# Spreading 1/den for every attention block by DMA turns instead of a matmul with a constant

## Chip, cores, metric

One core of one Trainium2 chip. The metric is the device time of one execution in microseconds (us). The kernel before takes 1090.96 us (median of 3 runs, 1089.22 to 1092.67). Engines: PE is TensorE, PEld its weight load, DVE VectorE, ACT ScalarE, POOL GpSimd, SP the engine that issues most DMAs.

## The reference

Four residual layers, bf16, 2048 tokens of width 512 (linear attention, gated MLP, linear attention, gated MLP, the two kinds with shared weights), forward and all gradients. What the change touches is the division by `den`:

```python
def _A_ref(x, wqkv, wo):                     # 32 heads of 16
    q, k, v = ...                            # x @ wqkv
    pq, pk = phi(q), phi(k)                  # where(t > 0, t + 1, exp(t)) + 1e-6
    kv = einsum("bhsd,bhse->bhde", pk, v); z = einsum("bhsd->bhd", pk)
    num = einsum("bhqd,bhde->bhqe", pq, kv)
    den = einsum("bhqd,bhd->bhq", pq, z)[..., None] + 1e-6
    return (num / den)... @ wo
x = x + _A_ref(_layernorm(x), ...)           # layer 0
x = x + _B_ref(_layernorm(x), ...)           # layer 1: (sigmoid(x wg) * (x wu)) wd
...                                          # layers 2 and 3 again, then jax.vjp for all gradients
```

## The kernel before

The tokens lie in 8 blocks of 256. The second pass of an attention layer (`a_p2`) makes, for each block, `den` (32 heads for each token), its reciprocal, the reciprocal spread over the 16 elements of each head and turned to have channels in partitions, the product `pnT = pqT * 1/den` (and `rphiT` for the gradient), then `ya = pnT @ Wp`. `Wp` is the product of the layer's `kvT` and `wo`, needed by all blocks.

There are two ways to spread. Blocks 0 and 1 of layers 0 and 2 (`RDMA = (2, 2)`) go over PE; blocks 2 to 7 go over DMA:

```python
    def den():
        ...                                             # 8 small matmuls into PSUM, + EPS into dn
        if by_dma:
            nc.vector.reciprocal(r[:], dn[:])
            for j in range(2):                          # cast and spread over the 16 elements of a head
                st["rx", j] = s1(k, "rx")
                ...
                if l == 0: nc.scalar.copy(dst, src)
                else:      nc.gpsimd.tensor_copy(dst, src)
            return
        nc.vector.reciprocal(r[:], dn[:])
        st["rr"] = rr = k.rr[k.rr_i % 2]                # bf16 high part and remainder, side by side
        nc.vector.tensor_copy(rr[:, :, 0:H], r[:])
        nc.vector.tensor_tensor(rr[:, :, H:2 * H], r[:], rr[:, :, 0:H], ALU.subtract)

    def turn():                                         # PE path: two transposes, one DVE copy
        for j in range(2):
            nc.tensor.transpose(tps[:, j, :], st["rr"][:, j, :], k.ident[:])
        nc.vector.tensor_copy(st["rT"][:], flat(tps[:]))

    def turn_by_dma(j):                                 # DMA path
        if j == 0: st["rT"] = t2(k, "rTx", [P, 2, NDC, P])
        nc.sync.dma_start_transpose(out=st["rT"][:, j, :, :], in_=st["rx", j][:])

    def spread(hf):                                     # PE path: r_ps is in PSUM
        for c2 in range(2):
            nc.tensor.matmul(ps[:, c2, :], lhsT=k.spread[:, 2 * hf + c2, :], rhs=st["rT"][:], ...)
        nc.vector.tensor_tensor(A.pn[b][:, sl, :], pq[:, sl, :], ps[:], ALU.mult)
        nc.vector.tensor_scalar(ph[:], flat(pq[:, sl, :]), -EPS, 1.0, ALU.add, ALU.min)
        nc.vector.tensor_tensor(flat(A.rphi[b][:, sl, :]), ph[:], flat(ps[:]), ALU.mult)

    def spread_turned(hf):                              # DMA path: the same three with rT in SBUF
        nc.vector.tensor_tensor(by_tile(A.pn[b]), by_tile(A.pq[b]), rT, ALU.mult)
        ...
```

The order of instructions on every engine is not written by hand. A planner builds it before the launch: each piece of work has a priority, the longest way from it to the end, plus an offset from a table; a model of the engines and buffers then gives each free engine its best ready piece. Its estimate of a step:

```python
    HOP = dict(PE=0.25, A=0.14, V=0.14, P=0.14, D=2.2)
    LAP = 0.08
    ...
        u.post = [(e, c if e == "D" else c - self.LAP, marks(m)) for e, c, m in u.post]
    ...
            u.prio += self.offsets.get(...)             # the table OFFSETS, 132 entries
```

## Time and profile before

| | before |
|---|---|
| time, us | 1090.96 |
| span of the profiled execution | 1090.0 |
| PE busy | 97% |
| DVE busy | 59% |
| PE time lost (waits and slow clock) at the start of layer 0's second pass, 45 to 76 us | 5.7 us (worked out below) |

The page, the stretches and the chain are in the prediction. Two more views matter later. First, what PE waits for between 40 and 80 us in the kernel before (waiting line, releaser: us in all, times, longest):

```profile
PE hT_ps L490 <- ACT h L555: 1.3, 1, 1.3
PE ya_ps L926 <- DVE rphiT L919: 1.3, 2, 1.1
```

The waits are several and short: for a DVE product, then for the layer norm `h` of layer 1. Second, where `Wp` is begun (the matmuls of `wp_ps` between 52 and 66 us: shortest, median, longest in ns, first and last start):

```profile
L751 PE MATMUL wp_ps<-wo,kvT x4: 377/379/379, 54.2 to 55.6; 128*128 128x512 bf16 x4
```

**A measure of lost time.** The records of PE's matmuls are incomplete (7292 of 7388 in this trace), so PE's busy time can be off by several us. The weight loads are complete, and each names its matmul. I therefore give every matmul the time it takes at full rate (0.109 us for 256 columns: eight take 0.88 us in the chain) and call the rest of any stretch *lost*: waits and slow clock together. The kernel before has 1055.7 us of work and 34.3 us lost. A recount with slightly different times for the short matmuls moves single entries of the tables below by up to 0.7 us and the differences between two rows by at most 0.4, mostly 0.2.

### The profile page before, as it was taken

The page shows a single profiled execution, that of the slowest core. Times are in us where ns is not written, and L with a number is a line of the kernel's source. Part 1 is how long each engine was busy: PE and PEld are TensorE (multiplying, and loading weights), DVE is VectorE, ACT ScalarE, POOL GpSimd, SP SyncE. Part 2 cuts the span into 40 slices and gives each one's busy share as a digit, 9 for nine tenths or more (in the row PEclk, how much of TensorE's full clock was granted, in tenths as well). Part 3 has the DMA queues.
Part 4 walks back from the last instruction along what each step waited for, and adds up shares of the span by engine and source line. Part 5 has one row for each costly group of instructions (what it writes and reads, how often), then busy time and mean ns, then how long its engine had stood idle before and what let it go on. Part 6 is the DMA issues. An engine that isn't in the chain of part 4 may idle for free.

```text
span 1090.0 us, 19650 instructions
## 1 busy us (share of the span) xinstructions
PE 1057.6 (97%) x7292; PEld 694.3 (64%) x7388; DVE 641.5 (59%) x1571; ACT 357.3 (33%) x713; POOL 184.8 (17%) x459
## 2 busy tenths in 40 slices
PE   6989999999999999999899999989999999999998
PEld 3657667677666766675556556655554466666787
DVE  6797786799885778787767657877755000000010
ACT  6665564455333433232234434331111000000010
POOL 4146675524402112000000000000000000000000
PEclk9999999999999999999999999999999999999999
DMA  7749879997999898866999799789999999999980
GB/s 247 258 136 289 247 221 258 261 206 180 214 225 217 224 213 190 193 160 157 238 249 255 216 272 273 207 191 225 236 264 259 269 233 211 207 235 235 203 184 21
DMA packets 503857, 239.29 MB, mean 220 GB/s; under 512 B 329456, under 2 KB 488912, under 8 KB 501712
## 3 DMA queue, kind: packets, MB, share of 16 engines
q1 hardware_dynamic: 503760, 238.02, 88.1%
q8 instruction: 58, 0.95, 0.4%
q14 instruction: 39, 0.32, 0.1%
HBM read 61.93 MB, written 95.72 MB: 145 GB/s over the span
## 4 chain that ended last, share of the span: by engine, by line
PE 88%; DVE 4%; DMA 3%; ACT 2%; issue 1%; POOL 1%; SPq 1%; DVEq 0%; ACTq 0%
PE dw_ps L1831 25%; PE dh_acc L1349 7%; PE dha_ps L1218 7%; PE dhh_ps L1277 6%; PE g_ps L1277 6%; PE u_ps L1277 6%; PE dh_acc L1347 6%; PE y_ps L1469 3%; PE y_acc L1319 3%; PE m_ps L1061 2%; PE dpk_ps L1202 2%; PE ya_ps L926 2%; PE dpn_ps L1000 2%; PE q_ps L815 2%; PE g_ps L643 2%; PE k_ps L617 2%
## 5 line engine op out<-in xcount | busy, mean ns | idle before, releaser
L1831 PE MATMUL dw_ps<-dw_set,h 128*128 128x352 bf16 (+2 forms) x1536 | 205.6, 297 | 0.0
L1831 PEld LDWEIGHTS <-h 128*128 128x128 bf16 x1536 | 150.3, 98 | 55.3
L1813 DVE TENSOR_SCALAR dw_o<-dw_ps 128x512 bf16<-128x512 f32 (+3 forms) x33 | 17.5, 540 | 225.6 <-PE dw_ps L1831 181.9
L1349 PE MATMUL dh_acc<-wgT,dg 128*128 128x512 bf16 x344 | 130.4, 379 | 2.1 <-DVE dg L1421 0.6
L1347 PE MATMUL dh_acc<-wuT,du 128*128 128x512 bf16 x331 | 125.4, 379 | 0.4
L1811 ACT ACTIVATE dw_o<-dw_ps 128x512 bf16<-128x512 f32 (+4 forms) x34 | 16.3, 481 | 246.5 <-PE dw_ps L1831 218.7
L1156 POOL TENSOR_SCALAR ab<-c 128x2 f32<-128x2 f32 x64 | 20.5, 320 | 430.5 <-DVE lnb_j L1153 424.4
L1277 PE MATMUL g_ps<-hT,wg 128*128 128x256 bf16 x704 | 92.9, 273 | 0.2 <-DMA hT<-h_d 0.2
L1277 PE MATMUL u_ps<-hT,wu 128*128 128x256 bf16 x704 | 92.5, 273 | 0.0
L1277 PE MATMUL dhh_ps<-gT,wdT 128*128 128x256 bf16 x704 | 88.9, 273 | 0.8 <-ACT gT L492 0.7
L1277 PEld LDWEIGHTS <-wg 128*128 128x128 bf16 x704 | 68.5, 98 | 21.2 <-DMA hT<-h_d 0.7
L1831 PE MATMUL dw_ps<-g,dw_set 128*128 128x512 bf16 (+1 forms) x343 | 77.1, 379 | 2.6 <-DMA dw_set<-hh_d 1.8
L1277 PEld LDWEIGHTS <-wdT 128*128 128x128 bf16 x704 | 68.4, 98 | 13.8 <-issue 1.0
L1277 PEld LDWEIGHTS <-wu 128*128 128x128 bf16 x704 | 68.9, 98 | 8.0
L1831 PEld LDWEIGHTS <-dw_set 128*128 128x128 bf16 (+1 forms) x352 | 35.1, 100 | 41.1 <-DMA dw_set<-hh_d 2.1
L1349 PEld LDWEIGHTS <-dg 128*128 128x128 bf16 x352 | 34.4, 98 | 36.2 <-DVE dg L1421 1.4
L1347 PEld LDWEIGHTS <-du 128*128 128x128 bf16 x352 | 34.4, 98 | 34.5 <-DVE du L1522 0.3
L1150 ACT ACTIVATE lnb_t<-dha_ps,rstd 128x512 f32<-128x512 f32 x32 | 22.0, 688 | 100.9 <-PE dha_ps L1218 50.6
L1402 ACT ACTIVATE th<-g_ps 128x512 f32<-128x512 f32 (+1 forms) x48 | 26.8, 558 | 69.6 <-PE g_ps L1277 61.9
L1522 DVE TENSOR_TENSOR du<-s2tl,dhh 128x512 bf16<-128x512 bf16 (+1 forms) x48 | 19.0, 401 | 43.5 <-ACT dhh L1517 37.2
L1308 DVE SCALAR_TENSOR_TENSOR hh<-th,u_ps 128x512 bf16<-128x512 f32 (+1 forms) x48 | 30.5, 639 | 22.9 <-ACT th L1303 16.8
L1319 PE MATMUL y_acc<-wd,hh 128*128 128x512 bf16 x166 | 40.4, 379 | 0.5
(204 smaller groups left out, 1805.9 us busy)
## 6 DMA issues: line engine op xcount, KB each, us to landing
s2t_d<-s2t SPq DMA_DIRECT2D x8, 1408.0 KB, 6.9
s2tl<-s2t_d SPq DMA_DIRECT2D x8, 1408.0 KB, 7.8
hh_d<-hh SPq DMA_DIRECT2D x16, 640.0 KB, 4.7
du_d<-du SPq DMA_DIRECT2D x80, 128.0 KB, 2.9
dg_d<-dg SPq DMA_DIRECT2D x80, 128.0 KB, 2.9
h_d<-h SPq DMA_DIRECT2D x32, 256.0 KB, 2.8
h<-h_d SPq DMA_DIRECT2D x18, 256.0 KB, 4.7
pk_d<-pk SPq DMA_DIRECT2D x16, 256.0 KB, 3.1
```

The costliest lines, as they stand in the source:

```text
L617: nc.tensor.matmul(ps[:], lhsT=A.hT[b][:, m, tslice(j)], rhs=k.wk[:, m, :], start=(m == 0), stop=(m == NDC - 1))
L643: nc.tensor.matmul(ps[:], lhsT=k.h[l, bb][:, j, cslice(m)], rhs=A.pk[bb][:, j, :], start=(first and i == 0), stop=(last and i == len(its) ...
L1150: nc.scalar.activation(t[:], dh_ps, ACT.Identity, scale=rs, accum_out=c12[:, 0:1])
L1218: nc.tensor.matmul(ps[:], lhsT=lh[:, c, tslice(j)], rhs=rh[:, c, :], start=(i + c == 0), stop=(i == 2 and c == NDC - 1))
L1277: nc.tensor.matmul(ps[:, i, :], lhsT=w[:, m, fsl(fc)], rhs=rhsT[:, m, :], start=(m == 0), stop=(m == NDC - 1))
L1308: nc.vector.scalar_tensor_tensor(hh, th[:, 0:w], 1.0, flat(up[:])[:, 0:w], ALU.add, ALU.mult)
L1319: nc.tensor.matmul(st["acc"][j][:], lhsT=st["hh"][:, fc, tslice(j)], rhs=k.wd[:, fc, :], start=(fc == 0), stop=(fc == NFC - 1))
L1347: nc.tensor.matmul(acc[j][:], lhsT=du[:, i, tslice(j)], rhs=k.wuT[:, fc, :], start=(fc == 0), stop=False)
L1349: nc.tensor.matmul(acc[j][:], lhsT=dg[:, i, tslice(j)], rhs=k.wgT[:, fc, :], start=False, stop=(fc == NFC - 1))
L1402: nc.scalar.activation(th[:, 0:w], flat(gp[:])[:, 0:w], ACT.Tanh, scale=0.5)
L1469: nc.tensor.matmul(ps[:], lhsT=st["hh"][:, fc, tslice(j)], rhs=k.wd[:, fc, :], start=(fc == 0), stop=(fc == NFC - 1))
L1831: nc.tensor.matmul(ps, lhsT=lhs(s_), rhs=rhs(s_), start=(s_ == 0), stop=(s_ == 31))
```

## The change

The intent is to use one way for all blocks: fewer PE and DVE instructions, no PSUM for the spread, and the room of the constants for two more buffers. The diff, cut to its core (parts that switch off a projection by tile and drop a dependency that no block has are left out, they act on nothing here):

```diff
-BUFS = dict(xb=5, w11=6, w4=7, t2=20, hh=2, pair=3, th=2, s1=6, lnf=2, accf=1)
+BUFS = dict(xb=5, w11=6, w4=7, t2=21, hh=2, pair=3, th=2, s1=7, lnf=2, accf=1)
-RDMA = (2, 2)
 OFFSETS = """
-    DE0:2=-86,3=-93,7=+11 DK0:4=+21 DP0:1=-15,2=+49,3=+75,4=-148,5=-40 ...
+    DE0:3=-81,7=+11 DE2:1=+97 DH2:1=+84 DK0:4=+21 DK2:4=-48 DP0:1=-15,2=+49,3=+71
     ... (most entries differ)
-    k.hs = consts.tile([P, NDC, P], BF16, name="hs")
-    k.spread = consts.tile([P, NDC, P], BF16, name="spread")
-    k.rr = [consts.tile([P, 2, P], BF16, name=f"rr{i}") for i in range(2)]
+    k.hs = consts.tile([P, NDC, H], BF16, name="hs")
-def build_spread(k): ...                 # four transposes and a copy
-def a_p2(k, l, b, xin_fn, deps, late, by_dma):
+def a_p2(k, l, b, xin_fn, deps):
-        if by_dma: ... return            # the DMA path is now the only one
-        st["rr"] = ...                   # the PE path: rr, turn, spread with r_ps
-        G.add("RT" + n, turn, 2 * C128, ["DE" + n, "SPREAD"] + late, [("V", 0.29, "-tp +rT")], "+tp -rr")
```

More of the change, by code (lines that the diff above doesn't have):

```diff
@@ L282 @@
 PULL = (10.0, 10.0, 10.0)
-AHEAD2, AHEAD3 = (2, 3), (2, 0)
+AHEAD2, AHEAD3 = 2, 2
 TURN = (6, 1, 1)
@@ L288 @@
 KEEPX, KEEPQ = 3, 2
-RDMA = (2, 2)
-SBT = range(8)
+SBT = {2: range(8), 0: range(0), 1: range(0)}
 SUMS = {1: ([0, 1], -1), 3: ([2, 3], 1), 5: ([4, 5], 3), 6: ([6], 5), 7: ([7], 6)}
@@ L294 @@
 OFFSETS = """
-    DE0:2=-86,3=-93,7=+11 DK0:4=+21 DP0:1=-15,2=+49,3=+75,4=-148,5=-40 DP2:0=-18,2=+21,4=+10,5=+30,6=-51 DT0:+67
-    DW1:1=-49,2=-2,3=-1,5=-8,6=-55 DW3:0=+39,1=+64,3=-2,4=-2,7=+23 Fg3:11=+27 G1:0=-27 G11:5=-36,7=+2
-    G3:0=+2,1=-5,4=+65,7=+119 GS0:2=+3,3=+14,4=-9,6=-39 GS2:6=+84,7=+19 J1:0=+59 K0:2=+92,5=-4,7=-14 K2:2=+31
-    LB1:3=+121 LB3:7=+72 LDH0:2=-3 LDH2:6=-2 LDL0:0=+102,2=+35,5=+36,6=+36,7=+51 LDL2:0=-71,1=-60 LDP0:1=+45,7=-7
-    LDX0:4=-5,5=+1 LG3:0=+67,1=+48 LN0:7=-144 LN2:7=-83 LN_0:5=+193 LN_2:7=+7 LP2:0=+83,7=+94 LQ2:4=+56 LS1:1=-38
-    LT3:4=-20 LX0:4=+83,5=+42,7=+76 MS0:1=-1,5=-276 MS2:1=-29,7=-37 Q0:1=-63,4=-161,5=-30,6=-98,7=+69 Q2:2=-11,3=-9
-    RT0:0=-112 RX0:4=+18 RX2:2=+55 S28:-25 S3:+20 SH0:4=-42 SO3:7=-91 SP2:3=+103 SPK2:4=-28 SPREAD:-254 SQ2:6=-17
-    SU1:0=-9,1=+8,5=+8 SU3:0=+19 SV3:7=+92 TB1:0=-27,5=-8 TG0:1=+2,2=+6,4=-129,5=-67 TG2:1=+11
-    TK0:0=+72,1=+129,2=+596,5=+343 TR1:5=-6 U0:0=+35 WGT:-13 WGTZ:-46 Y1:4=-9 Y33:1=-29,3=-2,4=-36
-    YA0:0=-115,4=+2,6=+12 ZE0:0=-12,1=-2,2=+43 ZE2:0=+68,1=+71,2=+88,3=+108,4=+183,5=+141,7=+75
+    DE0:3=-81,7=+11 DE2:1=+97 DH2:1=+84 DK0:4=+21 DK2:4=-48 DP0:1=-15,2=+49,3=+71
+    DP2:0=-18,2=+21,3=+4,4=+10,5=+30,6=-198 DT0:+67 DW1:1=-50,3=-1 DW3:0=+95,1=+64,4=-2,7=+13 Fg3:11=+28 Fh1:12=-14
+    Fh3:4=-25 G1:0=-49,1=-15 G11:7=+97 G3:4=+64,5=+66,7=+38 GS0:2=+20,5=+17,6=-68 GS2:6=+30 K0:0=-18 K2:2=+31
+    LB3:4=-3,7=+65 LDH2:6=+11,7=+11 LDL0:5=+36 LDL2:1=-69,2=-7,7=+23 LDP2:6=+2 LDQ2:6=-3 LDX0:4=-5 LG3:0=+58,1=+39
+    LN0:2=-53,4=-92,7=-170 LP0:2=-11,3=-11 LQ2:2=-2,3=-15,5=+7 LS1:1=-7 LX:7=+127 LX0:4=+76,5=+35 MS0:5=-306
+    MS2:1=-65,3=-1 Q0:1=-63,4=-40,5=-57,7=+64 Q2:2=+18 RX2:2=+69 S1:-43 S30:-17 SG2:-21 SH3:7=-73 SK2:7=-70 SM2:-73
+    SN0:2=-193,5=-178,6=-178 SN2:0=-118 SO3:7=-56 SPK2:3=+30 SQ0:1=+127,2=+8 SQ2:7=-122 SU1:5=+8 SV1:1=-89
+    SV3:0=+40,7=-139 TB1:5=-12 TG0:1=+2,2=+6,4=-176,5=-76,6=+6 TG2:4=+100,6=+71 TK0:0=+111,4=+293,5=+613,7=+151
+    U0:1=-40 WP2:3=+87 WT2:3=-45 Y1:4=-9 Y33:0=-16,1=-13 YA2:5=+8,6=-1 ZE0:2=+19
+    ZE2:0=+69,1=+72,2=+89,3=+160,4=+184,5=+142,6=+105 ZS0:3=+16,5=+30 ZS2:7=+28
 """
@@ L307 @@
 TOKENS = dict(mm=5, acc=2, tp=1, t2=BUFS["t2"], xb=BUFS["xb"], s1=BUFS["s1"], w4=BUFS["w4"], w11=BUFS["w11"],
-              hh=BUFS["hh"], th=BUFS["th"], pr=BUFS["pair"], lnf=BUFS["lnf"], accf=1, ln=4, dn=2, rr=2, rT=2)
+              hh=BUFS["hh"], th=BUFS["th"], pr=BUFS["pair"], lnf=BUFS["lnf"], accf=1, ln=4, dn=2)
 @with_exitstack
@@ L447, in build_consts @@
                             base=15, pattern=[[16, 8], [0, 16]], channel_multiplier=-1)
-    k.hs = consts.tile([P, NDC, P], BF16, name="hs")
-    nc.gpsimd.memset(k.hs[:], 0.0)
-    for o in (0, H):
-        v = k.hs[:, :, o:o + H]
-        nc.gpsimd.memset(v, 1.0)
-        nc.gpsimd.affine_select(out=v, in_=v, compare_op=ALU.is_ge, fill=0.0,
-                                base=0, pattern=[[128, NDC], [-16, H]], channel_multiplier=1)
-        nc.gpsimd.affine_select(out=v, in_=v, compare_op=ALU.is_ge, fill=0.0,
-                                base=15, pattern=[[-128, NDC], [16, H]], channel_multiplier=-1)
-    k.spread = consts.tile([P, NDC, P], BF16, name="spread")
-    k.rr = [consts.tile([P, 2, P], BF16, name=f"rr{i}") for i in range(2)]
-    for r in k.rr:
-        nc.gpsimd.memset(r[:], 0.0)
-    k.rr_i = 0
+    k.hs = consts.tile([P, NDC, H], BF16, name="hs")
+    nc.gpsimd.memset(k.hs[:], 1.0)
+    nc.gpsimd.affine_select(out=k.hs[:], in_=k.hs[:], compare_op=ALU.is_ge, fill=0.0,
+                            base=0, pattern=[[128, NDC], [-16, H]], channel_multiplier=1)
+    nc.gpsimd.affine_select(out=k.hs[:], in_=k.hs[:], compare_op=ALU.is_ge, fill=0.0,
+                            base=15, pattern=[[-128, NDC], [16, H]], channel_multiplier=-1)
     k.rstd = [consts.tile([P, 2 * NBLK], F32, name=f"rstd{l}") for l in range(4)]
@@ L469, in build_consts @@
     k.rstdh = {l: consts.tile([P, 2 * NBLK], F32, name=f"rstdh{l}") for l in (1, 3)}
-def build_spread(k):
-    nc = k.nc
-    ps = tpps(k, [P, NDC, P], "spread_ps")
-    for c in range(NDC):
-        nc.tensor.transpose(ps[:, c, :], k.hs[:, c, :], k.ident[:])
-    yield
-    nc.vector.tensor_copy(k.spread[:], ps[:])
 def flat(ap3):
@@ L744, in zz @@
         A.Z = k.p1.tile([P, NDC, H], BF16, name=f"Z{l}", tag="Z", bufs=1)
-        nc.vector.tensor_tensor(A.Z[:], k.hs[:, :, 0:H], A.z[:].unsqueeze(2).to_broadcast([P, NDC, H]), ALU.mult)
+        nc.vector.tensor_tensor(A.Z[:], k.hs[:], A.z[:].unsqueeze(2).to_broadcast([P, NDC, H]), ALU.mult)
     def wp(c):
@@ L852, in den, with turn @@
         yield
-        if by_dma:
-            r = k.p1.tile([P, 2, H], F32, name="rcp", tag="rcp", bufs=2)
-            nc.vector.reciprocal(r[:], dn[:])
-            for j in range(2):
-                yield
-                st["rx", j] = s1(k, "rx")
-                src = r[:, j, :].unsqueeze(2).to_broadcast([P, H, D // H])
-                dst = st["rx", j][:].rearrange("p (h e) -> p h e", h=H)
-                if l == 0:
-                    nc.scalar.copy(dst, src)
-                else:
-                    nc.gpsimd.tensor_copy(dst, src)
-            return
         r = k.p1.tile([P, 2, H], F32, name="rcp", tag="rcp", bufs=2)
         nc.vector.reciprocal(r[:], dn[:])
-        yield
-        st["rr"] = rr = k.rr[k.rr_i % 2]
-        k.rr_i += 1
-        nc.vector.tensor_copy(rr[:, :, 0:H], r[:])
-        yield
-        nc.vector.tensor_tensor(rr[:, :, H:2 * H], r[:], rr[:, :, 0:H], ALU.subtract)
-    def turn():
-        tps = tpps(k, [P, 2, P], "rT_ps")
-        for j in range(2):
-            nc.tensor.transpose(tps[:, j, :], st["rr"][:, j, :], k.ident[:])
-        yield
-        st["rT"] = k.p1.tile([P, TB], BF16, name="rT", tag="rT", bufs=2)
-        nc.vector.tensor_copy(st["rT"][:], flat(tps[:]))
-    def turn_by_dma(j):
+        for j in range(2):
+            yield
+            st["rx", j] = s1(k, "rx")
+            src = r[:, j, :].unsqueeze(2).to_broadcast([P, H, D // H])
+            dst = st["rx", j][:].rearrange("p (h e) -> p h e", h=H)
+            if l == 0:
+                nc.scalar.copy(dst, src)
+            else:
+                nc.gpsimd.tensor_copy(dst, src)
+    def turn(j):
         if j == 0:
@@ L886, in turn_by_dma, with spread @@
         nc.sync.dma_start_transpose(out=st["rT"][:, j, :, :], in_=st["rx", j][:])
-    def spread_turned(hf):
+    def spread(hf):
         if hf == 0:
@@ L902, in spread_turned @@
         nc.vector.tensor_tensor(rphi, rphi, rT, ALU.mult)
-    def spread(hf):
-        if hf == 0:
-            A.pn[b] = t2(k, "pnT")
-            A.rphi[b] = t2(k, "rphiT")
-        pq = A.pq[b]
-        ps = mmps(k, [P, 2, TB], "r_ps")
-        for c2 in range(2):
-            nc.tensor.matmul(ps[:, c2, :], lhsT=k.spread[:, 2 * hf + c2, :], rhs=st["rT"][:], start=True, stop=True)
-        yield
-        sl = slice(2 * hf, 2 * hf + 2)
-        nc.vector.tensor_tensor(A.pn[b][:, sl, :], pq[:, sl, :], ps[:], ALU.mult)
-        yield
-        ph = s1(k, "phq")
-        nc.vector.tensor_scalar(ph[:], flat(pq[:, sl, :]), -EPS, 1.0, ALU.add, ALU.min)
-        yield
-        nc.vector.tensor_tensor(flat(A.rphi[b][:, sl, :]), ph[:], flat(ps[:]), ALU.mult)
     def y(j):
@@ L933, in a_p2 @@
         G.load("LX" + n, lx, BLK if l == 0 else 2 * BLK, [f"YA{l}.{b - 2}.1"] + ([f"SX1.{C}"] if l else []) + deps, "+t2" if l == 0 else "+xb")
-    if by_dma:
-        eng = "P" if l else "A"
-        G.add("DE" + n, den, 8 * 0.027, [f"Q{n}.0", f"Q{n}.1", f"ZZ{l}", f"<YA{l}.{b - 2}.1"],
-              [("V", 0.22, "+dn -tp"), ("V", 0.55, "-dn"), (eng, 0.65, "+s1 @0"), (eng, 0.65, "+s1")], "+tp")
-        for j in range(2):
-            G.load(f"RX{n}.{j}", lambda j=j: turn_by_dma(j), BLK, [f"DE{n}" + ("" if j else "@0")] + ([f"~RX{n}.0"] if j else []), "-s1" if j else "+t2 -s1", turn=True)
-        for hf in range(2):
-            G.add(f"SP{n}.{hf}", lambda hf=hf: spread_turned(hf), 0.0, [f"RX{n}.{j}" for j in range(2)] + ([f"~SP{n}.0"] if hf else []),
-                  [("V", 0.42, "@pn"), ("V", 0.29), ("V", 0.42)], "" if hf else "+t2 +t2")
-        G.free("-t2", [f"SP{n}.{hf}" for hf in range(2)])
-    else:
-        G.add("DE" + n, den, 8 * 0.027, [f"Q{n}.0", f"Q{n}.1", f"ZZ{l}", f"<YA{l}.{b - 2}.1"],
-              [("V", 0.22, "+dn -tp"), ("V", 0.55), ("V", 0.2, "+rr"), ("V", 0.22, "-dn")], "+tp")
-        G.add("RT" + n, turn, 2 * C128, ["DE" + n, "SPREAD"] + late, [("V", 0.29, "-tp +rT")], "+tp -rr")
-        for hf in range(2):
-            G.add(f"SP{n}.{hf}", lambda hf=hf: spread(hf), 2 * C256, ["RT" + n] + ([f"<SP{n}.0"] if hf else []),
-                  [("V", 0.68, "@pn"), ("V", 0.29, "+s1"), ("V", 0.68, "-s1 -mm")], "+mm" if hf else "+mm +t2 +t2")
+    eng = "P" if l else "A"
+    G.add("DE" + n, den, 8 * 0.027, [f"Q{n}.0", f"Q{n}.1", f"ZZ{l}", f"<YA{l}.{b - 2}.1"],
+          [("V", 0.22, "+dn -tp"), ("V", 0.55, "-dn"), (eng, 0.65, "+s1 @0"), (eng, 0.65, "+s1")], "+tp")
+    for j in range(2):
+        G.load(f"RX{n}.{j}", lambda j=j: turn(j), BLK, [f"DE{n}" + ("" if j else "@0")] + ([f"~RX{n}.0"] if j else []), "-s1" if j else "+t2 -s1", turn=True)
+    for hf in range(2):
+        G.add(f"SP{n}.{hf}", lambda hf=hf: spread(hf), 0.0, [f"RX{n}.{j}" for j in range(2)] + ([f"~SP{n}.0"] if hf else []),
+              [("V", 0.42, "@pn"), ("V", 0.29), ("V", 0.42)], "" if hf else "+t2 +t2")
+    G.free("-t2", [f"SP{n}.{hf}" for hf in range(2)])
     pn = [f"SP{n}.{hf}@pn" for hf in range(2)]
-    if not by_dma:
-        G.free("-rT", [f"<SP{n}.1"])
     G.free("-t2", [f"SP{n}.0", f"SP{n}.1"])
@@ L1028, in a_b1 @@
               + ([f"CA{n}.0"] if j else []), [("A", 0.62)], "" if j else "+t2")
-    if l == 2 and b in SBT:
+    if b in SBT[l]:
         def turn(j):
             if j == 0:
-                st["gTt"] = t2(k, "gT2", [P, 2, NDC, P])
+                st["gTt"] = t2(k, f"gT{l}", [P, 2, NDC, P])
                 st["gT"] = lambda m: st["gTt"][:, :, m, :]
@@ L1077, in a_b1 @@
                   "+mm" + (" +accf" if b == 1 and m == 0 else " +w4" if b == NBLK - 1 and m == 0 else ""), pull=pull)
-        G.free(" ".join(["-t2"] * 2 * len(bs)), [f"<MS{n}.3"] + [("" if l and bb in SBT else "<") + f"TG{l}.{bb}.1" for bb in bs])
+        G.free(" ".join(["-t2"] * 2 * len(bs)), [f"<MS{n}.3"] + [("" if bb in SBT[l] else "<") + f"TG{l}.{bb}.1" for bb in bs])
 def a_bbarrier(k, l):
@@ L1277, in proj, with proj_tiles @@
             nc.tensor.matmul(ps[:, i, :], lhsT=w[:, m, fsl(fc)], rhs=rhsT[:, m, :], start=(m == 0), stop=(m == NDC - 1))
+    return ps
+def proj_tiles(k, w, rhsT, p, name):
+    nc = k.nc
+    ps = mmps(k, [P, 2, TB], name)
+    for i, fc in enumerate(pair_chunks(p)):
+        for m in range(NDC):
+            nc.tensor.matmul(ps[:, i, :], lhsT=w[:, m, fsl(fc)], rhs=rhsT[:, :, m, :], start=(m == 0), stop=(m == NDC - 1))
     return ps
@@ L1513, in chunk @@
         cs = slice(2 * p, 2 * p + len(pair_chunks(p)))
-        dps = proj(k, k.wdT, st["gT"], p, "dhh_ps")
+        dps = (proj_tiles if b in SBT[l] else proj)(k, k.wdT, st["gT"], p, "dhh_ps")
         yield
@@ L1529, in glu_bwd, with turn @@
               "" if j else "+th" if b < 2 else "+hh" if b in (2, 4) else "+t2" if b > 5 else "")
-    add_turn(k, "TB" + n, lambda: k.g1[b], lambda t: st.__setitem__("gT", t), "gT1", [[f"CB{n}.{j}", f"<G1{l}.{b - 1}.1"] for j in range(2)], PULL[2])
+    tb = [[f"CB{n}.{j}", f"<G1{l}.{b - 1}.1"] for j in range(2)]
+    if b in SBT[l]:
+        def turn(j):
+            if j == 0:
+                st["gT"] = t2(k, "gT1", [P, 2, NDC, P])
+            nc.sync.dma_start_transpose(out=st["gT"][:, j, :, :], in_=k.g1[b][:, j, :])
+        for j in range(2):
+            G.load(f"TB{n}.{j}", lambda j=j: turn(j), BLK, tb[j] + ([f"~TB{n}.0"] if j else []), "" if j else "+t2", PULL[2], True)
+    else:
+        add_turn(k, "TB" + n, lambda: k.g1[b], lambda t: st.__setitem__("gT", t), "gT1", tb, PULL[2])
     for p in range(NPAIR):
@@ L1616, in sweep1 @@
     G.load("WO", lambda: load_w4(k, k.w["wo"], "wo"), 2 * BLK, ["LX.5", "WV"], "+w4")
-    G.add("SPREAD", lambda: build_spread(k), 4 * C128, ["K0.3.1"], [("V", 0.6, "-tp")], "+tp")
     G.free("-w4", ["<K2.%d.1" % last])
@@ L1637, in sweep2 @@
     for b in range(NBLK):
-        a_p2(k, 0, b, lambda b=b: xin(b), [f"LN2.{b - 3}.1@h", f"<G1.{b - AHEAD2[0]}.0"], [f"<G1.{b - AHEAD2[0]}.{AHEAD2[1]}"], b >= RDMA[0])
+        a_p2(k, 0, b, lambda b=b: xin(b), [f"LN2.{b - 3}.1@h", f"<G1.{b - AHEAD2}.0"])
         layernorm(k, 1, b, lambda b=b: k.x[0, b], [[f"YA0.{b}.{j}"] for j in range(2)], b >= SUMMED[0])
@@ L1680, in sweep3 @@
     for b in range(NBLK):
-        a_p2(k, 2, b, lambda b=b: xin(b), [f"<Y33.{b - 3}.1", f"<G3.{b - AHEAD3[0]}.0"], [f"<G3.{b - AHEAD3[0]}.{AHEAD3[1]}"], b >= RDMA[1])
+        a_p2(k, 2, b, lambda b=b: xin(b), [f"<Y33.{b - 3}.1", f"<G3.{b - AHEAD3}.0"])
         layernorm(k, 3, b, lambda b=b: k.x[2, b], [[f"YA2.{b}.{j}"] for j in range(2)], b >= SUMMED[2])
```

## The prediction

> **What bounds the kernel now.** I read the page first. TensorE (PE) is busy 97% of the span, VectorE (DVE) 59%:
>
> ```profile
> span 1090.0 us, 19650 instructions
> PE 1057.6 (97%) x7292; PEld 694.3 (64%) x7388; DVE 641.5 (59%) x1571; ACT 357.3 (33%) x713; POOL 184.8 (17%) x459
> ```
>
> So PE has 1090.0 - 1057.6 = 32.4 us without work. Next I asked where these lie: busy time by engine in 40 slices (columns: length, then PE, weight load, DVE, ACT, POOL busy, granted clock, DMA share, GB/s). Three slices hold half of it:
>
> ```profile
> 0.00:27.20 27.20, 17.72 (x116) 9.35 (x119) 17.60 (x53) 18.92 (x31) 13.28 (x47) 1.00 0.79 248
> 54.50:81.80 27.30, 23.50 (x190) 16.17 (x192) 26.28 (x68) 17.00 (x34) 11.42 (x33) 0.94 0.47 136
> 1062.80:1090.00 27.20, 24.20 (x222) 21.43 (x220) 1.53 (x4) 1.54 (x4) 0.00 (x0) 0.99 0.07 21
> ```
>
> The first (9.5 us: first load, first layer norm) and the last (3.0 us: the closing drain) aren't touched by the change. The second is the start of attention layer 0's second pass, where the change acts. There DVE, not PE, is full (26.28 of 27.30), PE lacks 3.8 us, and it is the only slice with a dented clock. I narrowed it:
>
> ```profile
> 54.40:68.70 14.30, 10.57 (x93) 7.32 (x92) 14.24 (x40) 8.39 (x17) 3.69 (x12) 1.00 0.35 100
> 68.00:70.00 2.00, 1.59 (x8) 0.81 (x10) 2.00 (x6) 1.61 (x4) 0.00 (x0) 0.74 0.62 125
> 70.00:72.00 2.00, 2.00 (x14) 0.92 (x13) 1.77 (x5) 1.30 (x3) 0.39 (x2) 0.50 0.72 223
> 72.00:74.00 2.00, 2.00 (x19) 1.70 (x18) 2.00 (x8) 1.37 (x4) 1.77 (x5) 0.90 1.00 300
> ```
>
> For 14.3 us DVE is busy 14.24 us while PE does 10.57. After that idling the clock falls to 0.74, 0.50 and 0.90: a loss of 2 x (0.26 + 0.50 + 0.10) = 1.7 us of full-speed PE. The chain that ended last (start, length, what) agrees; from 54.9 to 68.7 it is all DVE apart from issue gaps, and the spread's own instructions are in it:
>
> ```profile
> 56.96 0.20 DVE rT L881
> 58.55 0.68 DVE pnT L914
> 59.64 1.19 DVE rphiT L919 x2
> 62.17 0.10 DVE rr L871
> 62.87 0.14 DVE rr L873
> 67.26 0.59 DVE rphiT L919
> 68.71 0.82 PE ya_ps L926 x2
> ```
>
> The same place in layer 2 differs. At 232 to 252 us PE does 19.50 of 20.00, because early down-projection work of layer 3 (dhh_ps) fills the waits. There PE is the bound, with DVE close behind (19.22).
>
> **What the Trainium skill says.** "VectorE: DVE Perf Modes", section "The perf-mode tier table": a tensor_tensor on bf16 in SBUF runs in a 2x mode, with any PSUM operand in 1x. The trace agrees for 128x512: the two products that read r_ps take 676 and 672 ns, those that read the turned tile in SBUF 417 and 416:
>
> ```profile
> L914 DVE TENSOR_TENSOR pnT<-pqT,r_ps x8: 668/676/686, 57.9 to 250.1; 128x512 bf16<-128x512 bf16 x8
> L897 DVE TENSOR_TENSOR pnT<-pqT,rTx x24: 361/417/420, 72.3 to 425.5; 128x512 bf16<-128x512 bf16 x24
> L886 SPq DMA_TRANSPOSE rTx<-rx x24: 1188/1209/1606, 66.9 to 421.3; - x24
> DMA to landing us min/median/max: 2.4/2.4/3.7
> ```
>
> "TensorE: Matmul & The Clock Gate", section "Part 1: The HAM clock gate": half clock is the default and sustained activity releases it. The dip to 0.50 after the idle stretch agrees. "DMA: Bandwidth & Descriptors", section "DMA Transpose (X-bar)": plain DMA turns are issued only from SP or ACT. Here all 24 sit on SP's queue, so new ones stand in line there.
>
> **The change part by part.** Blocks 2 to 7 of both attention layers already spread 1/den by DMA; the change moves blocks 0 and 1 of each, four blocks. The new "sweep by tile" projection, layer 1's DMA turn and the layer-0 turn are switched off by empty ranges, and the "late" dependency named blocks that don't exist for b < 2, so dropping it does nothing.
>
> *PE.* A block loses two transposes and four 256-column matmuls. In the chain four transposes take 0.22 us and eight such matmuls 0.87, so 0.11 + 0.44 = 0.55 us a block, 2.2 for four; building the spread constant takes four more transposes, 0.22. Sum 2.4 us. Only layer 2's half (1.1) and the constant (0.2) lie where PE is the bound: 1.3 us. Layer 0's 1.1 only enlarges the gap that DVE leaves.
>
> *DVE.* A block loses the cast (182 ns) and subtraction (212) into rr, the copy to rT (289) and four PSUM products (2 x 676 + 2 x 672): 3.38 us. It gains four SBUF products (2 x 417 + 2 x 416): 1.67 us. The reciprocal and the clamps of 277 ns stay. Net 1.71 us a block, 3.4 us for layer 0, where the chain is DVE end to end. I count that in full. In layer 2 the other 3.4 us lies beside PE.
>
> *ACT, POOL.* Two casts of 612 ns a block: 2.4 us on ACT in layer 0 (8.39 of 14.30 busy, so there is room), 2.4 us on POOL in layer 2 (nearly empty). The dropped POOL constants lie in the first 4.4 us under the first load, which lands at 4.16: no gain.
>
> *SP and DMA.* Eight turns of 1.21 us, 9.7 us of SP, four in each layer. In layer 0 the DMA share is 0.35, so they move freely.
>
> *Latency.* From the end of the reciprocal a turned block needs 0.61 (first cast) + 1.21 (first turn issued) + 2.4 (second lands) + 0.83 (two products) = 5.1 us. Now block 0's reciprocal ends at 53.2 and pnT at 59.2: 6.0 us, because each DVE step queues. So the path isn't longer, unless the turn meets the kvT turn that SP issues at 53.82 (1.29 us). I charge 0.5 us.
>
> *Buffers.* Dropped per partition: hs 768 bytes, spread 1024, two rr 1024, two rT 1024, in all 3840; one t2 (2048) and one s1 (1024) are added. A turned block holds one more t2 and two s1, so these mostly pay for themselves. In return two PSUM tiles a block are freed.
>
> *Priorities.* Most of the offset table is new: the order of pieces on every engine shifts over the whole kernel. Some 4.9 us of PE idle at 520 to 550 and 4.3 at 725 to 770 (waits for loads and turns) could shrink or grow. I choose -1 us, since a table is presumably retuned for the faster schedule, with about 4 us of spread either way.
>
> Sum: -1.3 (PE) - 3.4 (DVE stretch) - 0.9 (half of the clock dip's 1.7) + 0.5 - 1.0 = -6.1 us: 1090.96 becomes about 1085.
>
> **The rivals.**
> *A, only PE's own work counts:* PE is 97% busy and the PE path is pure PE overhead, so -2.4 us, 1088.5. For it: the page's totals. Against it: at the one place where PE isn't the bound, the removed DVE work sits in the chain.
> *B, the turn becomes the new wait:* at the start of a layer no earlier block covers the latency, and 5.1 us replaces the PE path. In layer 2 SP is held from 230.92 to 239.57 by the turn of the gate weights and from 242.90 for 5.68 us by WpT, so RX can land late. For it: PE spread was kept for just these blocks. Against it: den_ps of block 0 is ready at 51.8 in layer 0, and in layer 2 other PE work is at hand. If the turn costs 3 us in each layer, the time is 1091.
> *C, the removed wait returns elsewhere:* with the DVE stretch shorter, PE waits for the next thing (layer norm into hT: 1.3 us idle at 66.7 already). Then half of the 3.4 us and all of the dip's gain are lost: 1087.6.
> *D, the new order decides:* its gain or loss over 1000 us outweighs the four blocks: 1080 to 1094.
>
> **Range and chances.** The centre is 1085.0. Rivals A to C sit at 1088 to 1091, a good new table at about 1080; I take 1079.0 to 1091.0 as 8 in 10. A gain over 2% would mean under 1069: of the 32.4 us idle, 12.5 are start and end, so 19.9 + 2.4 would have to go nearly whole. A loss over 2% (over 1112.8) would need a long stall. Chances: 0.01 faster, 0.98 same, 0.01 slower.
>
> **What would show it.** PE busy near 1055 (1057.6 - 2.4, less some of the dip); r_ps, rT_ps and spread_ps gone, 32 rTx turns; DVE total down by about 6.8 us; in the 14 us after Wp of layer 0, PE idle under 2 us instead of 3.7 and no clock at 0.50. Wrong if that stretch is as long as before with PE waiting for rTx (B) or for h (C), or if the difference arises after 260 us (D).

## The result, and the profile after

| | before | after |
|---|---|---|
| median of 6 runs, us | 1091.29 (1089.22 to 1092.96) | 1088.06 (1086.3 to 1091.62) |
| ratio of the same rounds | | 0.9976, 95% interval 0.9955 to 0.9997 |
| profiled span, us | 1090.0 | 1084.6 |

A ratio is the mean time of one kernel's fast runs over that of the other's in the same rounds, so not quite the ratio of the medians. 0.9976 is 2.6 us less, where 6 were forecast. The same file run again gave 0.9959 (4.5 us). The profiled execution after was the fastest of its six, so the 5.4 us between the two spans flatter the change.

The page after:

```profile
span 1084.6 us, 19597 instructions
PE 1055.2 (97%) x7265; PEld 692.1 (64%) x7360; DVE 637.3 (59%) x1558; ACT 358.0 (33%) x717; POOL 186.7 (17%) x457
```

There are 28 weight loads fewer. Twelve of them are for matmuls of 128 columns and sixteen for 256, 2.4 us at the full rate given above, as forecast (2.4); the sums of the tables below have 2.6 (1053.1 against 1055.7). DVE fell by 4.2 us, not by 6.8; the overlap of DVE instructions, shown below, explains a part of this, the rest was not followed up. Lost time by stretch, from the weight loads (us; with the trace of the second run of the same file, to show what repeats):

```
              0-45  45-76  76-228  228-265  265-515  515-770  770-end   all
before        11.3    5.7     2.4      1.4      0.4      9.6      3.5  34.3
after         12.0    4.7     1.0      2.8      0.3      6.8      3.9  31.5
after, again  11.6    4.8     1.2      2.8      0.4      6.7      5.3  32.9
```

So layer 0's start (45 to 76 us) lost only 1.0 us less, of which the new order had already lost 0.7 (0.3 in the second run) more before 45 us; layer 2's start (228 to 265) lost 1.4 us more; and the rest comes from stretches without a spread. The stretches of the prediction, after (length, then PE, PEld, DVE, ACT, POOL busy with counts, granted clock, DMA share, GB/s; the last three are cut where PE's waits begin and end):

```profile
54.40:68.70 14.30, 11.90 (x97) 7.82 (x95) 14.28 (x39) 10.61 (x22) 3.97 (x13) 0.92 0.62 173
...
57.34:62.75 5.41, 5.35 (x51) 3.94 (x52) 5.41 (x15) 3.83 (x8) 0.46 (x3) 1.00 0.58 158
62.75:65.74 2.99, 0.86 (x8) 0.52 (x7) 2.99 (x9) 2.97 (x7) 2.63 (x8) 1.00 0.23 45
65.74:72.26 6.52, 5.85 (x42) 3.64 (x43) 5.41 (x19) 4.54 (x10) 3.53 (x12) 0.74 0.78 186
```

Two of the same stretches in the kernel before:

```profile
57.34:62.75 5.41, 4.27 (x44) 2.91 (x43) 5.41 (x14) 1.31 (x3) 0.00 (x0) 1.00 0.56 194
62.75:65.74 2.99, 2.59 (x25) 2.08 (x23) 2.99 (x11) 2.77 (x7) 1.89 (x6) 1.00 0.00 0
```

DVE is as full as ever (14.28 of 14.30). PE is now busy without a break up to 62.75, then does 0.86 us in 3. The clock falls after that hole as it fell before: 0.74 for 6.52 us is 1.7 us of full-speed PE, the same loss as in the prediction. PE's waits between 40 and 80 us, after:

```profile
PE hT_ps L472 <- ACT h L537: 2.1, 1, 2.1
PE den_ps L829 <- ACT hT L474: 0.7, 1, 0.7
```

The several waits for DVE have become one of 2.1 us for the layer norm's `h`. The chain that ended last shows what leads to it (start, length, what):

```profile
55.01 0.69 DVE kvT L723
...
56.09 1.21 DVE pqT L582 x2
...
57.34 0.38 PE wp_ps L733
...
58.19 1.75 PE q_ps L797 x16
...
60.20 1.46 PE ya_ps L873 x6
...
61.85 0.90 PE q_ps L797 x8
...
62.77 0.60 ACT phi_e L578
...
63.98 0.51 ACT rx L843
64.49 0.50 ACT phi_e L578
64.98 0.71 ACT h L537
...
65.74 0.40 PE hT_ps L472 x4
```

Before, this chain was DVE from 54.9 to 68.7. Now it is DVE up to 57.3, PE to 62.75, ACT to 65.7, PE again. No turn is in it: block 0's products are done at 55. But `Wp` begins later than before:

```profile
L733 PE MATMUL wp_ps<-wo,kvT x4: 376/376/379, 56.5 to 57.8; 128*128 128x512 bf16 x4
```

That is 56.5 against 54.2 us. Two things hold `kvT`, from which `Wp` is made, and they end within 0.1 us of each other. On DVE it now stands behind block 0's products, done at 54.98. And it needs `kv_ps`, which PE begins 2.2 us later than before and ends at 54.91, because the new order puts 16 more matmuls of `q_ps` (1.75 us) ahead of it (before, then after):

```profile
51.61 1.05 PE L737 MATMUL kv_ps<-GTb,wv 128*128 128x128 bf16 x16
53.85 1.06 PE L719 MATMUL kv_ps<-GTb,wv 128*128 128x128 bf16 x16
```

The first gate matmul of layer 1, which ends the stretch, starts at 70.35 instead of 71.71 (second run 70.31): 1.4 us earlier, about the size of layer 0's share of the removed PE work and the spread constant, 1.3 us.

### The profile page after: what moved, and what is told of

Its sections match the earlier page's. It is cut to its first block, busy times and chain, and to the rows that moved or that the text cites. A ratio compares the mean times of both kernels' runs of the same rounds, so it can differ in the third digit from the quotient of the medians.

```text
span 1084.6 us, 19597 instructions
## 1 busy us (share of the span) xinstructions
PE 1055.2 (97%) x7265; PEld 692.1 (64%) x7360; DVE 637.3 (59%) x1558; ACT 358.0 (33%) x717; POOL 186.7 (17%) x457
## 4 chain that ended last, share of the span: by engine, by line
PE 83%; DVE 5%; DMA 3%; issue 1%; POOL 1%; SPq 1%; ACT 1%; DVEq 0%; ACTq 0%; POOLq 0%
PE dw_ps L1786 25%; PE dha_ps L1155 7%; PE g_ps L1214 6%; PE dh_acc L1296 6%; PE u_ps L1214 6%; PE dhh_ps L1214 6%; PE dh_acc L1294 6%; PE y_acc L1266 3%; PE y_ps L1416 3%; PE dpk_ps L1139 3%; PE m_ps L998 2%; PE ya_ps L873 2%; PE dpn_ps L937 2%; PE k_ps L599 1%; PE g_ps L625 1%
## 5 line engine op out<-in xcount | busy, mean ns | idle before, releaser
L1294 PE MATMUL dh_acc<-wuT,du 128*128 128x512 bf16 x324 | 122.8, 379 | 0.3
```

Source lines behind the costliest of these rows:

```text
L1294: nc.tensor.matmul(acc[j][:], lhsT=du[:, i, tslice(j)], rhs=k.wuT[:, fc, :], start=(fc == 0), stop=False)
```

## The experiments

Each kernel was run in five rounds against the kernel before on the same chip. Lost time by stretch, as above (the three runs in which the planner's table is empty have other stretches and are left out):

```
                 work    span   0-45  45-76  76-228  228-265  265-515  515-770  770-end   all
frozen_switch  1053.1  1095.3   12.2    8.3     2.1      5.7      0.4      9.5      4.1  42.2
switch_only    1053.3  1092.5   11.7    6.5     2.1      5.5      1.7      8.0      3.6  39.2
old_table      1053.0  1102.1   12.0    8.3     2.9      4.2      2.4     10.4      8.9  49.1
new_table_only 1055.7  1108.5   13.0    6.2     3.3      1.7      6.8     16.9      4.9  52.8
dve_minus      1055.7  1088.9   11.3    2.5     2.2      1.3      0.6     11.1      4.2  33.3
 ... again     1055.7  1088.6   13.3    2.8     1.7      1.4      0.7      9.0      4.0  32.9
dve_plus       1053.1  1091.6   12.6    9.6     0.0      3.6      0.7      8.4      3.6  38.5
rx_on_pool     1053.1  1086.1   12.2    5.3     1.1      2.6      0.3      6.6      5.0  33.0
after_less_dve 1053.1  1089.1   12.0    4.5     0.9      2.6     -0.2      7.8      8.5  36.1
after_less_act 1053.1  1084.6   11.8    5.0     0.9      2.6      0.1      6.2      5.0  31.5
..._less_both  1053.1  1085.6   12.5    3.5     1.0      2.8      0.1      9.2      3.4  32.5
```

Two of these traces are of a slow execution among their six: old_table (1103.86 us) and after_less_dve (1090.86 us, with 8.5 us lost at the end). Their late stretches are not typical.

Theory at first: the DVE relief is real, but the turn's latency (rival B) or the layer norm (rival C) takes it back. Rival: the switch does little, the new order does all (D).

### The parts of the change, one by one

**after_again**, the changed kernel unaltered.

> The changed kernel once more, unaltered, to narrow its ratio and to get a second trace of it. If its first trace (span 1084.6 us, 5.4 us under the kernel before) is typical, the ratio is near 0.995. If that trace was a lucky execution and only PE's own 2.4 us are saved, the ratio is near 0.9975.

Measured: 1086.3 us (1084.63 to 1088.16), ratio 0.9959 (0.9937 to 0.998).

**switch_only**, the kernel before with its own table and buffers:

```diff
-RDMA = (2, 2)
+RDMA = (0, 0)
```

> The kernel before with blocks 0 and 1 of both layers turned by DMA, old priorities, old buffer counts, constants kept. Theory 1 (the switch saves PE's 2.2 us, and the DVE relief in layer 0 is not cashed because PE then waits for something else): 1088 to 1089 us. Rival, the prediction's step (DVE relief in full): 1085 us. Rival, one more t2 and two more s1 held per block starve the schedule: over 1091 us.

Measured: 1096.39 us (1094.21 to 1098.2), ratio 1.0047 (1.0025 to 1.0069). The switch alone is slower, by 5 us.

**old_table**, the changed kernel with the old offsets.

> The changed kernel with the old offset table; the difference to the changed kernel is the worth of the new table with the code held. If the new table brings the 1 us that was predicted, this is 1 us slower than the changed kernel; if the table is what carries the change, it is 3 us slower or more; if the new table costs something, it is faster.

Measured: 1098.67 us (1097.14 to 1105.16), ratio 1.0085 (1.0056 to 1.0114).

**new_table_only**, the kernel before with the new offsets.

> The kernel before with the new offset table alone (spread on PE, old buffers). If priorities by themselves carry the gain: 1088 us. If the table fits only the schedule that it was made for: 1092 us or more.

Measured: 1109.25 us (1106.73 to 1110.22), ratio 1.0159 (1.0132 to 1.0185).

What follows: neither table fits the other code. The old table costs the new code some 12 us (against the median of after_again, of the same rounds), the new table costs the old code 17 (ratio 1.0159). The table is not a bonus on top of the switch (I had put it at -1 us); with the old table the switch is a loss.

### The switch without any change of order

`switch_only` still lets the planner move other pieces. **frozen_switch** keeps the order of the kernel before on every engine and exchanges the pieces in place: the two `rr` steps become the two casts, the two transposes two DMA turns, the four PSUM products SBUF products; the spread matmuls go. Its `rx` and `rTx` have buffers of their own (two and one); to make room, `dn` has one instead of two and the constants of the spread are gone.

```diff
+        if l in (0, 2):          # in den(), in place of the two rr steps
+            for j in range(2):
+                yield
+                st["rx", j] = ...; (nc.scalar.copy if l == 0 else nc.gpsimd.tensor_copy)(dst, src)
+            return
     def turn():
+        if l in (0, 2):
+            for j in range(2):
+                nc.sync.dma_start_transpose(out=st["rT"][:, j, :, :], in_=st["rx", j][:])
+            return
     def spread(hf):
+        if l in (0, 2):
+            yield; yield from spread_turned(hf); return
```

> The kernel before, its order of instructions on every engine kept, with the four blocks' spread done by DMA turn in the very places of the PE path (two PE transposes become two turns, the rr cast and subtraction become two casts on ACT or POOL, four PSUM products become SBUF products; 28 matmuls gone). Theory as predicted (what is removed is worth its time): about 1086 us. Rival now favoured (each saving needs another order: in the old one PE stands behind the turn): 1091 us or more, with PE waiting for pnT in layer 0 and in layer 2.

Measured: 1095.78 us (1092.58 to 1097.57), ratio 1.0045 (1.0031 to 1.0058). DVE is no longer full in the 14.3 us from 54.4 (11.42 us), and PE still waits. In the chain of waits stand the turns themselves:

```profile
57.37 2.47 DMA rTx<-rx
...
64.96 2.44 DMA rTx<-rx
```

and PE's waits in 40 to 80 us and, last line, in 235 to 262 us (layer 2):

```profile
PE hT_ps L477 <- ACT h L542: 2.0, 1, 2.0
PE ya_ps L933 <- DVE pnT L900: 1.4, 2, 1.0
...
PE ya_ps L933 <- DVE pnT L900: 1.8, 1, 1.8
```

The lost time is 2.6 us more in layer 0 (8.3 against 5.7) and 4.3 us more in layer 2 (5.7 against 1.4), which with 2.4 to 2.6 us less work leaves some 4.4 of the 5 us. This is rival B: in the old order the block's turn of about 2.5 us, and the casts before it, stand where PE has nothing else lined up. In layer 2 I had seen other PE work "at hand", but the order doesn't put it there. A part of layer 2's loss can come of the edit itself: there block 1's casts on POOL waited 4.3 us for the two `rx` buffers that block 0's turns still held. switch_only, which has the usual buffers but another order, lost nearly as much there (5.5 us).

### Is DVE the pace-setter at layer 0's start?

**dve_minus** is the kernel before with the order kept, but in layer 0 the eight products of blocks 0 and 1 read `pqT` in SBUF instead of `r_ps` (a wrong result):

```diff
+        by = pq[:, sl, :] if l == 0 else ps[:]
-        nc.vector.tensor_tensor(A.pn[b][:, sl, :], pq[:, sl, :], ps[:], ALU.mult)
+        nc.vector.tensor_tensor(A.pn[b][:, sl, :], pq[:, sl, :], by, ALU.mult)
```

(and the same for `rphiT`).

> The kernel before, order kept; in layer 0's blocks 0 and 1 the eight products read pqT (bf16, SBUF) in place of r_ps (PSUM), so each takes some 0.42 instead of 0.67 us: 2.1 us less DVE work at the stretch where DVE is full, nothing else changed. Wrong result on purpose. If a microsecond of DVE there is a microsecond of the kernel: 2 us less (1089 us), and the first g_ps of layer 1 starts 2 us earlier than at 71.7. If PE waits for the layer norm chain anyway: no change.

> A second trace and timing of the kernel before with cheaper products in layer 0 (wrong result on purpose). In the first trace PE was 3.3 us ahead from 121 to 724 us, and lost 2.3 of it at the loads of 733 to 785 us, while the mean time didn't change. If that loss is systematic, this trace loses it there too and the ratio stays at 1.000; if it was one execution's slow load, this trace keeps some 3 us and the two ratios average 0.998.

Measured: 1090.65 us (1088.3 to 1090.96), ratio 0.9998 (0.9986 to 1.001); again, 1088.91 us (1087.9 to 1090.31), ratio 0.9982 (0.9969 to 0.9994). Each product starts the next one 0.26 us sooner, so DVE has 2.1 us less to do, and the stretch lost 3.2 and 2.9 us less. The first gate matmul of the first run starts at 69.03 instead of 71.71 us. (The edit also frees the products from waiting for `r_ps`; DVE was idle for 0.06 of the 14.3 us in the kernel before, so this counts for little.) The dip of the clock is gone from both: in 54 to 82 us it is 1.00, against 0.94 in the kernel before, and PE does 25.76 us (second run 25.75) instead of 24.20:

```profile
54.00:82.00 28.00, 25.76 (x222) 18.43 (x221) 26.92 (x77) 19.82 (x40) 14.95 (x40) 1.00 0.51 145
```

So the reading of the prediction was right for the kernel before: DVE sets the pace there, and the relief comes back with the dip on top. It doesn't all reach the end: the first run lost 1.5 us more at loads of 515 to 770 us, the second 2.0 us more in the first 45 us. In time the runs gained 0.2 us, which is within the noise, and 2 us of the 3.

**dve_plus** does the opposite to the changed kernel: in layer 0's blocks 0 and 1 the product `pnT` is issued three times (the result stays right).

```diff
+        for _ in range(3 if l == 0 and b < 2 else 1):
             nc.vector.tensor_tensor(by_tile(A.pn[b]), by_tile(A.pq[b]), rT, ALU.mult)
```

> The changed kernel with its first product (pnT from pqT and the turned tile) issued three times in layer 0's blocks 0 and 1: 8 more DVE operations of 0.42 us, 3.3 us, same result, same order. If DVE still sets the pace from 54 to 69 us in the new order: the first g_ps of layer 1 starts some 3 us later than 70.3 and the kernel takes up to 3 us more. If the new order already did block 0's spread before the stretch, and PE waits there for the layer norm chain on ACT and POOL: under 1.5 us.

Measured: 1091.34 us (1089.36 to 1095.38), ratio 1.0004 (0.9985 to 1.0023), some 3 to 5 us over the changed kernel. The stretch lost 9.6 us instead of 4.7, and the first gate matmul starts at 75.88 us. At this point I read that as "DVE still sets the pace in the new order". The next runs correct this.

**rx_on_pool** moves the casts for the turn in layer 0's blocks 0 and 1 from ACT to POOL, in the changed kernel.

> The changed kernel with the casts of layer 0's blocks 0 and 1 issued on POOL in place of ACT, order of all else kept. ACT is 10.6 of 14.3 us busy in the stretch, up from 8.4. If these casts hold up the exponentials and layer norm on ACT: 0.5 to 1.5 us less before the first g_ps; if ACT had room, as predicted: no change within 0.3 us there.

Measured: 1088.65 us (1086.92 to 1092.8), ratio 0.9983 (0.9966 to 1.0); the stretch lost 5.3 us, 0.6 more, and the first gate matmul starts 0.7 us later (71.08), which neither guess had. The casts of these two blocks on ACT aren't the trouble by themselves. The run isolates less than it was meant to: POOL, which got the casts, also works on the layer norm.

### What holds the stretch in the new order?

Three runs that take work out of the changed kernel in layer 0's blocks 0 and 1, order kept (all with a wrong result). **after_less_dve** leaves out the four products `rphiT * 1/den`, **after_less_act** leaves out one of the two casts in each block (both turns read the first), **after_less_both** does both.

```diff
+        if l or b > 1:                                   # after_less_dve
             nc.vector.tensor_tensor(rphi, rphi, rT, ALU.mult)
+            if l == 0 and b < 2 and j == 1:              # after_less_act
+                st["rx", 1] = st["rx", 0]
+                return
             st["rx", j] = s1(k, "rx")
```

> The changed kernel, order kept, without the product rphiT x 1/den in blocks 0 and 1 of layer 0 (wrong gradients on purpose): four VectorE products fewer, about 1.35 us of occupied VectorE time. Theory 1, VectorE still sets the pace there (other VectorE work moved in): the first gate matmul of layer 1 comes 1.3 to 2 us earlier than at 70.35 us, time about 1.5 us under the changed kernel, 1086.5 beside a before of 1090.3, ratio about 0.9955. Theory 2, the layer norm's chain through ScalarE has taken over: first gate matmul within 0.5 us of 70.35, ratio like the changed kernel's, 0.996 to 0.998.

> The changed kernel, order kept, with one of the two casts for the turn left out in blocks 0 and 1 of layer 0 (both turns read the first, wrong result on purpose): 1.2 us of ScalarE work fewer. Theory 1 (VectorE): first gate matmul within 0.5 us of 70.35, time like the changed kernel's. Theory 2 (ScalarE and the layer norm's chain): 0.7 to 1.2 us earlier, and TensorE's wait for h at 65.7 us, 2.1 us, falls below 1.5.

> Both cuts at once. Theory 1: as after_less_dve. Theory 2: as after_less_act. If each waits for the other in turn, both together gain clearly more than the sum of the single ones: first gate matmul at 68 us or earlier and no clock dip between 66 and 72 us, time 2 to 3 us under the changed kernel.

Measured: 1088.12 us (1085.39 to 1090.86), ratio 0.9966 (0.9951 to 0.9981); 1086.7 us (1085.44 to 1087.69), 0.9955 (0.9942 to 0.9967); 1087.58 us (1086.73 to 1091.19), 0.9971 (0.9955 to 0.9987). None differs from the changed kernel's own 0.9976 and 0.9959. With 1.3 us of DVE work gone, the stretch loses 4.5 instead of 4.7 us, with ACT's work gone 5.0, and the first gate matmul starts at 70.14 and 70.36 us instead of 70.35. The 2.13 us wait for `h` is there in all three. The chain of after_less_dve shows why DVE's relief is worth next to nothing here:

```profile
54.01 0.91 PE kv_ps L719 x16
...
54.94 0.04 DVE kvT L723
...
57.28 0.38 PE wp_ps L733
```

Block 0's two products, half of the 1.3 us, are the ones that lie before `kvT`. DVE gets ahead by them and then sits idle for 0.53 us, waiting for PE, which does `kv_ps` until 54.92; from there it is as in the changed kernel, `wp_ps` at 57.28 instead of 57.34. PE and DVE are both filled up to here, so less work for DVE alone gains nothing and more work for it (dve_plus) costs. Theory 1 doesn't hold by itself.

Theory 2 was tested less than I meant. The casts of block 0 lie before 50 us, and block 1's second cast, the one taken out of the stretch, ran at 60.64; without it ACT sits idle there for 0.87 us instead of 0.31. In the hole from 62.75 to 65.74 ACT is busy 2.97 of 2.99 us, and the cast in it (63.88) is of block 2, which the change doesn't touch. POOL has what `h` needs at 64.07, but `h` starts at 64.88, behind that cast and an exponential in ACT's order. No run took work out of ACT there, so ACT's load in the hole stays a possible holder.

With both cuts the first gate matmul starts at 69.80 instead of 70.35, in an execution that began `kv_ps` 0.5 us late (54.38), and no clock dip appears: 1.2 us less lost in the stretch. One execution with a shifted start can't tell whether the cuts or the shift removed the dip; dve_minus_again too has a hole (0.66 us of PE work from 66 to 68 us) and keeps a clock of 1.00.

### The table and the buffers

Three kernels with an empty table ask what the change is worth to the bare planner.

```diff
-OFFSETS = """ ... """
+OFFSETS = ""
```

> The kernel before with an empty offset table: priorities from the dependency graph alone. It shows how much time the old table holds: 10 to 25 us slower than with it.

> The changed kernel with an empty offset table. Against the previous kernel it gives the switch and the buffers when neither side is tuned: 2 to 6 us faster than that if the switch is good in itself; equal or slower if only a table made for it makes it pay.

> The changed kernel with an empty table and the old buffer counts (20 and 6). Without tables, before was 1138.4 and after 1122.8 us. If the two buffers made that difference: near 1138; if the switch did: near 1123; a single order is one draw, so a few us either way mean little.

Measured: before_no_table 1138.42 us (1136.33 to 1139.95), ratio 1.0438; after_no_table 1122.81 us (1121.4 to 1126.23), 1.0301; no_table_old_buffers (the latter with `t2=20`, `s1=6`) 1145.67 us (1140.14 to 1147.74), 1.049. The table is worth 48 us to the old code (10 to 25 were expected) and 35 to the new. With the bare planner the change gains 15.6 us (2 to 6 expected), but the switch alone loses 6 to 7 and the two buffers gain 21 to 23 (by ratios or by medians; the last run is of other rounds and another chip). Each of these orders is one draw of a planner whose result jumps with small changes, so I take from this only that buffers can weigh more than the spread, not their size in the tuned kernel. What the two buffers bring there was not measured alone; a fair test needs a table tuned for 20 and 6.

## Why the prediction was wrong

**PE's work: right.** Forecast 2.4 us fewer, measured 2.4 to 2.6.

**The failed step: "Net 1.71 us a block, 3.4 us for layer 0, where the chain is DVE end to end. I count that in full", with half of the dip on it.** The stretch was to gain 3.4 + 0.9 - 0.5 = 3.8 us. It gained 1.4 us to the first gate matmul, of which PE's removed work alone is some 1.3: next to nothing of DVE's relief arrived. By the prediction's own marks: PE idle in the 14.3 us is 2.4 us (14.30 - 11.90), where under 2 was forecast, and the clock still falls to 0.52 between 68 and 70 us; it had named rival C for just this case. Three things were wrong in it.

*The size.* I added durations, but consecutive DVE instructions overlap. The DVE timeline of the kernel before (start, length):

```profile
57.95 1.28 DVE L914 TENSOR_TENSOR pnT<-pqT,r_ps 128x512 bf16<-128x512 bf16 x2
59.15 0.48 DVE L917 TENSOR_SCALAR phq<-pqT 128x512 bf16<-128x512 bf16 x2
```

Two products of 676 ns each hold the engine from 57.95 to 59.15, 0.60 us apiece: the next one starts 0.08 us before the recorded end. The planner's `LAP = 0.08`, which its estimate of a step takes off the duration, has the same size, and the Trainium skill ("Perfetto Trace Analysis", section "Optimizing Scalar/DVE Operations") says it too: of the overhead in a profiled DVE instruction about half, the write's acknowledgement, overlaps with the next one; it gives some 60 ns on SBUF, these products show 80. I passed over both. Counted from start to start, the two blocks lose 6.45 us (4.78 for the products, 0.80 clamps, 0.87 for `rr` and `rT`) and gain 3.50: 2.95, not 3.4.

*The turn.* I charged 0.5 us for its latency, once, because 5.1 us by the turn looked no longer than 6.0 by PE. In frozen_switch block 0's path took 6.6 us (from the end of the reciprocal at 54.10 to the end of the products `pnT` at 60.69): the casts stood between exponentials on ACT, and the turn, issued at 56.07, behind the `kvT` turn that the prediction had feared (54.67, 1.30 us). frozen_switch, which has the relief and the turn in the old order, lost 2.6 us more in layer 0, while dve_minus, with 2.1 us of relief and no turn, lost 3.2 us less. So in that order, by my estimate, the turn (with its casts) takes back between 4 and 6 us there: the 2.6 and 3.2 together, less up to 1.4 us by which the missing PE work alone widens the gap. Rival B was right for this order, and its guess of 3 us a layer was nearer than my 0.5.

*The end of the chain.* I took the order as given. The new table gets rid of the turn's wait by making block 0's `den` 5.6 us earlier (45.8 instead of 51.4 us) and its products 4.7 us earlier. In exchange `kvT` comes later, behind these products on DVE and behind 16 more matmuls of `q_ps` on PE, and `Wp` 2.3 us later. PE is then busy without a break to 62.75, and `h` starts only 0.9 us earlier than before (64.88, before 65.79). So DVE's relief doesn't shorten the stretch, and a hole of 2.1 us for `h`, with its clock dip, remains: rival C's picture. That a DVE busy 14.28 of 14.30 us sets the pace in the one order and not in the other is shown: dve_minus and after_less_dve told the two apart. What holds `h` is only narrowed down. The casts that the change adds to ACT don't (after_less_act, rx_on_pool); the chain passes through DVE, PE and ACT in turn, ACT is full at its end, and no run moved `kv_ps` forward or emptied ACT in the hole. This part of the cause stays open.

**Layer 2.** Forecast -1.1 us, PE's half. The work went, but the stretch lost 1.4 us more (2.8 against 1.4), so nothing is left. PE waits there 0.9 us for `h` and 0.7 for `hT`, and for no turn; why was not followed up. In the old order the stretch lost 4.3 us more, with the caveat about the buffers made above.

**The table: -1.0 us was no estimate.** Between 76 and 228 us the new order lost 1.4 us less. A wait of the kernel before that has nothing to do with the spread (at 155 to 160 us) is gone:

```profile
PE ya_ps L926 <- DVE pk L600: 1.7, 1, 1.7
```

Between 515 and 770 us it lost 2.8 us less, at loads whose waits differ by 1 to 3 us between executions of one order (dve_minus and its repetition: 11.1 and 9.0). Against the same code with the old table the new one is worth some 12 us; against the kernel before, the stretches without a spread lost 2.3 to 3.9 us less (next paragraph).

**The sum.** Change of time by trace, first and second run: PE work -2.6 and -2.6, lost up to the end of layer 0's stretch (0 to 76 us) -0.3 and -0.6, in layer 2's +1.4 and +1.4, everything else -3.9 and -2.3: -5.4 and -4.1 us. The timed runs say -2.6 and -4.5. The time lies close to rival A (1088.5), but not for A's reason alone: PE's work is a sure 2.4 to 2.6, lost time in the two stretches of the spread rises by about 1 us in sum, and the order adds what the execution lets it keep. That the total lies so near to A is in part luck.

## What to carry to other kernels

An engine that is full in a stretch is a candidate, not the pace-setter: take work out of it with the order kept, and see whether the next engine's wait ends sooner. When work moves from a short path on an engine to a DMA with a latency, count the relief and the latency in the same order of instructions; where the order is planned anew, ask what was pushed back to bring the turn forward. A tuned order belongs to its code: run new code with the old order to see the mechanism, and expect no more of it than that.

## What the Trainium skill lacked or had wrong

- "Perfetto Trace Analysis", section "Identifying the Most-Contended Engine", names the engine with the highest occupancy as the one to optimize first. The section after it has regimes that follow each other in time, but not a stretch in which two engines are full at once and the chain passes from one to the other: DVE is busy 14.28 of 14.30 us in the changed kernel, and 1.3 us less work for it moved the first gate matmul only from 70.35 to 70.14 us, while more work delayed it (75.88 in dve_plus).
- "DMA: Bandwidth & Descriptors", section "DMA Transpose (X-bar)", has constraints and alternatives, but no time for a small turn to set against the PE path; another page ("VectorE: DVE Perf Modes", section "The three transpose paths") has one figure for 128x128, and I found none for 128x512. Here a turn of 128x512 took 1.2 us to issue and 2.4 us to land, and in the chain of frozen_switch 2.47 and 2.44 us.
